# Gated product of a scan kernel: formed in token order in bf16 and transposed back, in place of an in-place fp32 product in PSUM

## The chip, the cores and the metric

One core of a Trainium2 chip runs the whole kernel. The metric is the device time of one execution in microseconds (us), the median of several. The profile is of one execution; its span is 1.7 to 1.8 us shorter than that execution's own time. PE is the matmul engine, DVE the vector engine, ACT the scalar engine with its function tables, POOL the general engine, SP the engine that issues most transfers.

## The reference, cut to what matters

```python
# x, r_gate, i_gate: (4, 6336, 256) fp32
a_t   = exp(8 * sigmoid(r_gate) * log(sigmoid(a_param)))
norm  = sqrt(max(1 - a_t * a_t, 1e-06))
x_gated = norm * sigmoid(i_gate) * x
for t in range(S):                       # one scan for each batch row and channel
    h = a_t[:, t] * h + x_gated[:, t]
    y[:, t] = h
# then: causal 5-tap convolution of y -> sigmoid gate; (gate * (y @ w_val)) @ w_out
```

The 25,344 tokens (4 x 6336) are cut into 51 tiles of up to 512 tokens and 28 chunks of up to two tiles. Inputs come with tokens on the partitions. The scan needs channels on the partitions and tokens along the free dimension, so something must be transposed; the change is about what, where and in which type.

## The kernel before

The parts that the change and the argument touch (cuts marked with `# ...`; h is one of two halves of the channels, k counts half chunks):

```python
UNITS = [1, 2, 2, 2, 2, 2, 3, 3, 2, 2, 2, 1, 1, 1, 2]   # chunks in one batch of square roots
OSB = "ADADAD..."   # who evicts output piece q from PSUM: D = DVE, A = ACT

def op_u2(g, eng):      # POOL: u = (tanh(i/2) + 1) * x, bf16, tokens on partitions
    # ...
def op_exp(k, eng):     # ACT: a = exp(..), read from PSUM transposed by PE, fp32
def op_e(k, eng):       # POOL: e = a * a
def op_sq(u, eng):      # ACT: norm = sqrt(0.25 - 0.25 e), bf16, one batch; needs another table
def op_uT(k, eng):      # PE: u transposed into the one fp32 PSUM buffer
    xg = psum.tile([P, CHUNK], FP32, name="xg", tag="xg", bufs=1)
    # ...
        nc.tensor.matmul(out=xg[:, o:o + (P - 1) * nj + 1:nj],        # stepped columns
                         lhsT=uring[:, g % NS, j, h * P:(h + 1) * P], rhs=ident_b[:], ...)
def op_xg(k, eng):      # DVE: product, in place
    nc.vector.tensor_tensor(out=xg[:, 0:nt], in0=xg[:, 0:nt], in1=nring[...], op=ALU.mult)
def op_scan(k, eng):    # DVE: reads a from SBUF and xg from PSUM, writes y
    nc.vector.tensor_tensor_scan(out=yring[...], data0=aring[...], data1=xg[:, c0:c1], ...)
```

Afterwards PE does the convolution (gp) and the value matmul (val), ACT the tanh of the gate (tg), DVE the gate product (gv), PE the output matmul (ops), and DVE or ACT the eviction (osb). A small list scheduler in the kernel (`make_plan`) fixes the order of all instructions from constants: a cost and a priority for each kind, the batches and the string of evictions. The change comes with its own set of these constants.

## Time and profile before

| | before |
|---|---|
| time, median of 3 | 351.11 us (350.84 to 351.58) |
| span of the profiled execution | 348.6 us |
| busy: ACT, DVE, POOL, PE | 310.3, 270.9, 266.6, 250.4 us |
| share of the load and store queue | 79.5% of 16 engines |

### The profile page before, as it was taken

How to read it: one execution, taken by the hardware profiler on the slowest of the kernel's cores; microseconds unless marked ns; L12 is line 12 of the kernel's file. 1: busy time of each engine (PE TensorE's matmuls, PEld its weight loads, DVE VectorE, ACT ScalarE, POOL GpSimd, SP SyncE). 2: the span in 40 equal slices, each digit the busy share in tenths (PEclk: the TensorE clock that was granted, in tenths of full speed). 3: DMA queues.
4: the chain of work that ended last, by engine and by line, in shares of the span. 5: the costliest groups of instructions: out<-in, count | busy, mean ns of one | idle time of the engine just before them, and what ended most of it. 6: DMA issues, size and time to landing. Idle time of an engine off the chain costs nothing.

```text
span 348.6 us, 6564 instructions
## 1 busy us (share of the span) xinstructions
PE 250.4 (72%) x2559; PEld 161.4 (46%) x2559; DVE 270.9 (78%) x247; ACT 310.3 (89%) x262; POOL 266.6 (76%) x170
## 2 busy tenths in 40 slices
PE   1162773796785986787687867849978866988884
PEld 0041441553453654554455554527545544555452
DVE  3031675587798899876989869976999989999992
ACT  6859999879899899889979989997999999999673
POOL 7788998999797997997799949967938965873200
PEclk9997598899897899998999989978999999999999
DMA  7997988895999978997999976996985996522324
GB/s 201 371 416 261 407 285 342 305 350 202 371 414 362 350 282 321 374 419 228 390 399 394 351 261 228 392 392 225 353 343 181 368 387 244 192 83 120 122 120 183
DMA packets 30797, 104.51 MB, mean 300 GB/s; under 512 B 4391, under 2 KB 4654, under 8 KB 30766
## 3 DMA queue, kind: packets, MB, share of 16 engines
q1 hardware_dynamic: 29390, 103.83, 79.5%
q0 software_dynamic: 1376, 0.26, 0.9%
q8 instruction: 20, 0.33, 0.4%
q14 instruction: 11, 0.09, 0.1%
HBM read 78.39 MB, written 25.95 MB: 299 GB/s over the span
## 4 chain that ended last, share of the span: by engine, by line
PE 31%; ACT 25%; DVE 16%; issue 13%; DMA 11%; POOL 2%; SPq 0%; DVEq 0%; ACTq 0%; POOLq 0%
PE gp L377 12%; PE xg L326 10%; DVE yring L351 8%; ACT tri L280 6%; DMA ri<-in_i_gate_dram 6%; ACT ering L315 5%; DVE xg L335 5%; ACT tg L385 4%; PE ops L415 4%; DMA wo<-in_moe_w_out_dram 4%; ACT L315 3%; PE val L393 3%; ACT L385 3%; PE srT L268 3%; ACT aring L302 2%
## 5 line engine op out<-in xcount | busy, mean ns | idle before, releaser
L310 POOL TENSOR_TENSOR ering<-aring 128x1024 f32<-128x1024 f32 (+2 forms) x56 | 94.5, 1694 | 45.1 <-ACT aring L302 42.6
L289 POOL TENSOR_TENSOR uring<-t,xt 128x1024 bf16<-128x1024 f32 (+1 forms) x51 | 117.0, 2294 | 4.2
L351 DVE TENSOR_TENSOR_SCAN yring<-aring,yring,xg 128x1024 bf16<-128x1024 f32 (+5 forms) x54 | 111.1, 2056 | 1.0
L280 ACT ACTIVATE tri<-ri 128x2048 bf16<-128x2048 f32 (+1 forms) x51 | 94.8, 1861 | 3.4 <-DMA ri<-in_i_gate_dram 3.3
L335 DVE TENSOR_TENSOR xg<-xg,ering 128x1024 f32<-128x1024 f32 (+2 forms) x56 | 62.0, 1107 | 43.3 <-PE xg L326 27.8
L326 PE MATMUL xg<-ident_b,uring 128*128 128x128 bf16 x396 | 58.8, 335 | 41.1 <-DVE yring L351 38.9
L377 PE MATMUL gp<-yring,diag 64*64 64x512 bf16 (+14 forms) x1164 | 72.0, 381 | 22.4 <-ACT tg L385 22.2
L302 ACT ACTIVATE aring<-srT,khf 128x1024 f32<-128x1024 bf16 (+2 forms) x56 | 62.0, 1108 | 9.4 <-PE srT L268 8.9
L326 PEld LDWEIGHTS <-uring 128*128 128x128 bf16 x396 | 44.4, 138 | 55.2 <-issue 44.1
L415 PE MATMUL ops<-wo,gv 128*128 128x256 bf16 x396 | 62.2, 279 | 10.5 <-DVE osb L426 5.1
L403 DVE SCALAR_TENSOR_TENSOR gv<-tg,val 128x1024 bf16<-128x1024 bf16 (+1 forms) x54 | 60.2, 1120 | 7.1 <-PE val L393 5.4
L287 POOL TENSOR_SCALAR t<-tri 128x1024 f32<-128x1024 bf16 (+1 forms) x51 | 52.0, 1019 | 11.9 <-ACT tri L280 10.5
L385 ACT ACTIVATE tg<-gp 128x1024 bf16<-128x1024 f32 (+1 forms) x51 | 51.0, 999 | 9.3 <-PE gp L377 8.9
L377 PEld LDWEIGHTS <-diag 64*64 64x64 bf16 x1164 | 32.3, 114 | 49.9 <-issue 36.8
L415 PEld LDWEIGHTS <-gv 128*128 128x128 bf16 x396 | 38.6, 105 | 32.1 <-issue 19.2
L393 PE MATMUL val<-yring,wv 128*128 128x512 bf16 (+1 forms) x204 | 51.8, 377 | 1.5 <-DVE gv L403 1.3
L315 ACT ACTIVATE ering<-ering,b 128x2048 bf16<-128x2048 f32 (+2 forms) x28 | 50.5, 1804 | 1.1
L268 PE MATMUL srT<-ident_b,tri 128*128 128x128 bf16 x396 | 35.1, 234 | 16.6 <-ACT aring L302 8.4
L426 DVE COPY osb<-ops 128x512 f32<-128x512 f32 x58 | 39.2, 676 | 7.6 <-PE ops L415 7.3
L268 PEld LDWEIGHTS <-tri 128*128 128x128 bf16 x396 | 28.8, 106 | 26.9 <-issue 13.7
L428 ACT COPY osb<-ops 128x512 f32<-128x512 f32 x41 | 24.0, 586 | 9.5 <-PE ops L415 9.2
L393 PEld LDWEIGHTS <-wv 128*128 128x128 bf16 x204 | 19.4, 99 | 16.8 <-issue 4.5
(29 smaller groups left out, 59.6 us busy)
## 6 DMA issues: line engine op xcount, KB each, us to landing
ri<-in_r_gate_dram SPq DMA_DIRECT2D x48, 512.0 KB, 6.2
ri<-in_i_gate_dram SPq DMA_DIRECT2D x48, 512.0 KB, 7.0
xt<-in_x_dram SPq DMA_DIRECT2D x48, 512.0 KB, 6.2
out_dram<-osb SPq DMA_DIRECT2D x48, 512.0 KB, 4.1
ri<-in_r_gate_dram SPq DMA_DIRECT2D x3, 256.0 KB, 3.1
ri<-in_i_gate_dram SPq DMA_DIRECT2D x3, 256.0 KB, 3.2
xt<-in_x_dram SPq DMA_DIRECT2D x3, 256.0 KB, 3.2
out_dram<-osb SPq DMA_DIRECT2D x3, 256.0 KB, 2.1
```

The costliest lines, as they stand in the source:

```text
L268: nc.tensor.transpose(out=dst[:, col:col + P], in_=src[:, j, h * P:(h + 1) * P], identity=ident_b[:])
L280: nc.scalar.activation(out=tri[:, :, 0:nj, :], in_=ri[:, :, 0:nj, :], func=ACT.Tanh, scale=0.5)
L289: nc.gpsimd.tensor_tensor(out=uring[:, g % NS, 0:nj, :], in0=t1[:, 0:nj, :], in1=xt[:, 0:nj, :], op=ALU.mult)
L310: nc.gpsimd.tensor_tensor(out=ering[:, h, a0:a0 + nt], in0=a, in1=a, op=ALU.mult)
L315: nc.scalar.activation(out=nring[:, :, 2 * a0:2 * a0 + nt], in_=ering[:, :, a0:a0 + nt], func=ACT.Sqrt, scale=-0.25, bias=b025[:, 0:1])
L326: nc.tensor.matmul(out=xg[:, o:o + (P - 1) * nj + 1:nj], lhsT=uring[:, g % NS, j, h * P:(h + 1) * P], rhs=ident_b[:], start=True, stop=True)
L335: nc.vector.tensor_tensor(out=xg[:, 0:nt], in0=xg[:, 0:nt], in1=nring[:, h, 2 * a0:2 * a0 + nt], op=ALU.mult)
L351: nc.vector.tensor_tensor_scan(out=yring[:, h, y0 + c0:y0 + c1], data0=aring[:, h, a0 + c0:a0 + c1], data1=xg[:, c0:c1], initial=0.0 if fr ...
L377: nc.tensor.matmul(out=gp[64 * h:64 * h + 64, m, c0:c1], lhsT=diag[rows, h, kk, rows], rhs=yring[rows, h, src:src + c1 - c0], start=(sh == 0),
L385: nc.scalar.activation(out=tg[:, :, 0:nt], in_=live.pop(("gp", g))[:, :, 0:nt], func=ACT.Tanh, scale=0.5)
L393: nc.tensor.matmul(out=val[:, m, 0:nt], lhsT=wv[:, hk, m * P:(m + 1) * P], rhs=yring[:, hk, y0:y0 + nt], start=(hk == 0), stop=(hk == H - 1))
L415: nc.tensor.matmul(out=ops[:, e, :], lhsT=gv[:, 2 * i + e, hk, :], rhs=wo2[:, hk, :], start=(hk == 0), stop=(hk == H - 1))
```

## The change

The intent is to shorten the product. The norm, computed with channels on the partitions, is transposed by PE to token order (bf16 in PSUM). There DVE multiplies it with u, bf16 with bf16 into bf16, a tile at a time. PE transposes the product back into bf16 PSUM, where the scan reads it. i and x must then be loaded with consecutive tokens on consecutive partitions, which turns runs of 4 KB in memory into runs of 1 KB. The batches of square roots are cut anew, the first of three chunks instead of one, the ring for y shrinks from 8 to 6 tiles, and evictions, costs and priorities are a new set.

```diff
-UNITS = [1, 2, 2, 2, 2, 2, 3, 3, 2, 2, 2, 1, 1, 1, 2]
+UNITS = [3, 1, 3, 3, 2, 3, 2, 3, 2, 2, 1, 1, 1, 1]
-NY = 8
+NY = 6
+NXG = 3
 # ... OSB: 41 evictions on ACT before, 32 after; COST and PRIO
-        for dst, src in ((ri[:, 0, 0:nj, :], rf), (ri[:, 1, 0:nj, :], if_), (xt[:, 0:nj, :], xf)):
-            nc.sync.dma_start(dst, src[t0:t0 + nt, :].rearrange("(p j) d -> p j d", j=nj))
+        nc.sync.dma_start(ri[:, 0, 0:nj, :], rf[t0:t0 + nt, :].rearrange("(p j) d -> p j d", j=nj))
+        for dst, src in ((ri[:, 1, 0:nj, :], if_), (xt[:, 0:nj, :], xf)):
+            nc.sync.dma_start(dst, src[t0:t0 + nt, :].rearrange("(j p) d -> p j d", p=P))
 # ... op_uT and the old op_xg go
+        def op_nT(g, eng):
+            # ...
+            nT = psum.tile([P, SUB, D], BF16, name="nT", tag="nT", bufs=1)
+                    nc.tensor.transpose(out=nT[:, j, h * P:(h + 1) * P],
+                                        in_=nring[:, h, n0 + j * P:n0 + (j + 1) * P], identity=ident_b[:])
+        def op_xg(g, eng):
+            xg = work.tile([P, SUB, D], BF16, name="xg", tag="xg", bufs=NXG)
+            nc.vector.tensor_tensor(out=xg[:, 0:nj, :], in0=live.pop(("nT", g))[:, 0:nj, :],
+                                    in1=uring[:, g % NS, 0:nj, :], op=ALU.mult)
+        def op_xT(k, eng):
+            xT = psum.tile([P, CHUNK], BF16, name="xT", tag="xT", bufs=1)
+            transposes(xT, [(live["xg", g], tiles[g][1] // P) for g in range(*chunks[c][2:])], h)
-                    ..., data1=xg[:, c0:c1],
+                    ..., data1=xT[:, c0:c1],
```

More of the change, by code (lines that the diff above doesn't have):

```diff
@@ L16 @@
 CHUNKS = [[256], [512]] + [[512, 512]] * 23 + [[512], [256], [256]]
-UNITS = [1, 2, 2, 2, 2, 2, 3, 3, 2, 2, 2, 1, 1, 1, 2]
+UNITS = [3, 1, 3, 3, 2, 3, 2, 3, 2, 2, 1, 1, 1, 1]
 NS = 10
-NY = 8
+NY = 6
 NIN = 3
 NTRI = 4
+NXG = 3
 NOSB = 3
-OSB = ("ADADADADDDDDDDDDDDDDDDDDDADADDDDDDDDADAAAADDDDDAADAADDDAADADDADADADADDAAAAADAAADADDADDDDAD"
-       "DAAAAAAAA")
+OSB = ("DDAADDDADDDDDDDDDDADADDDDDDDDADDADDDDDDDADDDDDDDADDDADDADAADADADADDDADDDDDADADADDAAAAAADDA"
+       "DDDDAAAAA")
 COST = dict(load=(0.1, 3.8), tanh=(0.2, 1.7), u2=(0.25, 3.15), srT=(0.05, 0.45), exp=(0.35, 0.86), e=(0.1, 1.8),
-            sq=(0.3, 1.71), uT=(0.1, 0.65), xg=(0.17, 1.07), scan=(0.21, 2.14), conv=(0.2, 1.1), tg=(0.19, 0.83),
+            sq=(0.3, 1.71), nT=(0.05, 0.47), xg=(0.1, 0.58), xT=(0.05, 0.45), scan=(0.21, 2.14), conv=(0.2, 1.1), tg=(0.19, 0.83),
             val=(0.02, 0.93), gv=(0.15, 1.07), out=(0.02, 0.47), osbD=(0.68, 0), osbA=(0.59, 0),
             store=(0.1, 1.2))
-PRIO = dict(load=5.13, store=-0.06, tanh=3.86, exp=-0.46, sq=-2, tg=-0.7, srT=0.17, uT=-2, conv=0.26, val=6,
-            out=-0.57, e=1.19, u2=4.62, xg=4.5, scan=6, gv=1.35, osb=-2)
+PRIO = dict(load=5.07, store=4.64, tanh=5.95, exp=3.94, sq=0.63, tg=0.73, srT=3.16, nT=4.77, xT=-1.91,
+            conv=3.92, val=4.01, out=-0.12, e=4.3, u2=4.55, xg=-0.64, scan=3.88, gv=4.0, osb=-0.43)
 TABLE, SEM, DMA_LAT = 1.3, 0.15, 2.2
@@ L93, in make_jobs @@
             + ([("srT", 2 * sh.chunk_of[g - NTRI] + 1)] if g >= NTRI else []))
-        job("u2", "POOL", f, [("tanh", g)] + ([("uT", 2 * sh.chunk_of[g - NS] + 1)] if g >= NS else []))
+        job("u2", "POOL", f, [("tanh", g)] + [("xg", g - NS)])
+        job("nT", "PE", f, [("sq", unit_of[c]), ("xg", g - 1)])
+        job("xg", "DVE", f, [("nT", g), ("u2", g)] + ([("xT", 2 * sh.chunk_of[g - NXG] + 1)] if g >= NXG else []))
         job("conv", "PE", f, [("scan", 2 * c + 1), ("tg", g - 1)])
@@ L109, in make_jobs @@
             job("e", "POOL", f, [("exp", k), aold])
-            job("uT", "PE", f, [("u2", g1 - 1), ("scan", k - 1)])
-            job("xg", "DVE", f, [("uT", k), ("sq", unit_of[c])])
-            job("scan", "DVE", f, [("xg", k), ("val", ylast - 1), ("conv", ylast)])
+            job("xT", "PE", f, [("xg", g1 - 1), ("scan", k - 1)])
+            job("scan", "DVE", f, [("xT", k), ("val", ylast - 1), ("conv", ylast)])
     for q, (g, i) in enumerate(sh.pieces):
@@ L316, in op_sq @@
                                      func=ACT.Sqrt, scale=-0.25, bias=b025[:, 0:1])
-        def op_uT(k, eng):
-            c, h = k // 2, k % 2
-            xg = psum.tile([P, CHUNK], FP32, name="xg", tag="xg", bufs=1)
-            g0, g1 = chunks[c][2:]
-            for g in range(g0, g1):
-                nj = tiles[g][1] // P
-                for j in range(nj):
-                    o = (g - g0) * WIN + j
-                    nc.tensor.matmul(out=xg[:, o:o + (P - 1) * nj + 1:nj],
-                                     lhsT=uring[:, g % NS, j, h * P:(h + 1) * P],
-                                     rhs=ident_b[:], start=True, stop=True)
-            live["xg", k] = xg
-        def op_xg(k, eng):
-            c, h = k // 2, k % 2
-            nt, a0 = chunks[c][1], shape.apos[c]
-            xg = live["xg", k]
-            nc.vector.tensor_tensor(out=xg[:, 0:nt], in0=xg[:, 0:nt], in1=nring[:, h, 2 * a0:2 * a0 + nt],
-                                    op=ALU.mult)
+        def op_nT(g, eng):
+            c = chunk_of[g]
+            n0 = 2 * shape.apos[c] + tiles[g][0] - chunks[c][0]
+            nT = psum.tile([P, SUB, D], BF16, name="nT", tag="nT", bufs=1)
+            for j in range(tiles[g][1] // P):
+                for h in range(H):
+                    nc.tensor.transpose(out=nT[:, j, h * P:(h + 1) * P],
+                                        in_=nring[:, h, n0 + j * P:n0 + (j + 1) * P], identity=ident_b[:])
+            live["nT", g] = nT
+        def op_xg(g, eng):
+            nj = tiles[g][1] // P
+            xg = work.tile([P, SUB, D], BF16, name="xg", tag="xg", bufs=NXG)
+            nc.vector.tensor_tensor(out=xg[:, 0:nj, :], in0=live.pop(("nT", g))[:, 0:nj, :],
+                                    in1=uring[:, g % NS, 0:nj, :], op=ALU.mult)
+            live["xg", g] = xg
+        def op_xT(k, eng):
+            c, h = k // 2, k % 2
+            xT = psum.tile([P, CHUNK], BF16, name="xT", tag="xT", bufs=1)
+            transposes(xT, [(live["xg", g], tiles[g][1] // P) for g in range(*chunks[c][2:])], h)
+            live["xT", k] = xT
         def yend(c):
@@ L348, in op_scan @@
             yp = yend(c) - 1
-            xg = live.pop(("xg", k))
+            xT = live.pop(("xT", k))
             for (c0, c1, fresh) in shape.segments(t0, nt):
                 nc.vector.tensor_tensor_scan(
-                    out=yring[:, h, y0 + c0:y0 + c1], data0=aring[:, h, a0 + c0:a0 + c1], data1=xg[:, c0:c1],
+                    out=yring[:, h, y0 + c0:y0 + c1], data0=aring[:, h, a0 + c0:a0 + c1], data1=xT[:, c0:c1],
                     initial=0.0 if fresh else yring[:, h, yp:yp + 1], op0=ALU.mult, op1=ALU.add)
@@ L436 @@
         ops_by_name = dict(load=op_load, tanh=op_tanh, u2=op_u2, srT=op_srT, exp=op_exp, e=op_e, sq=op_sq,
-                           uT=op_uT, xg=op_xg, scan=op_scan, conv=op_conv, tg=op_tg, val=op_val, gv=op_gv,
+                           nT=op_nT, xg=op_xg, xT=op_xT, scan=op_scan, conv=op_conv, tg=op_tg, val=op_val, gv=op_gv,
                            out=op_out, osb=op_osb, store=op_store)
```

## The prediction

> **What bounds the kernel now.** I read the page's first part, then the busy times by stretch, then the groups by shape, the waits, and last the chain in the stretch where the work of the vector engine looked tight. First the shares:
>
> ```profile
> span 348.6 us, 6564 instructions
> PE 250.4 (72%) x2559; PEld 161.4 (46%) x2559; DVE 270.9 (78%) x247; ACT 310.3 (89%) x262; POOL 266.6 (76%) x170
> ```
>
> ACT has least room: 38.3 us of idle in the span. The stretches (engine busy times in the order PE, PEld, DVE, ACT, POOL, then granted clock, DMA share, GB/s) tell when:
>
> ```profile
> 0.00:20.00 20.00, 3.63 (x19) 2.06 (x19) 4.87 (x20) 14.20 (x15) 14.03 (x21) 1.00 0.95 304
> 20.00:60.00 40.00, 21.30 (x180) 13.82 (x184) 18.37 (x17) 36.76 (x28) 37.58 (x22) 0.80 0.88 335
> ...
> 180.00:220.00 40.00, 31.81 (x359) 21.14 (x357) 35.16 (x29) 36.49 (x32) 33.36 (x20) 0.96 0.88 322
> 220.00:260.00 40.00, 31.27 (x313) 20.44 (x312) 35.19 (x27) 36.96 (x30) 28.46 (x18) 0.91 0.89 337
> 260.00:300.00 40.00, 31.45 (x361) 20.78 (x360) 37.41 (x30) 39.61 (x35) 30.38 (x18) 1.00 0.77 282
> 300.00:348.60 48.60, 38.72 (x414) 23.58 (x412) 40.07 (x43) 36.97 (x44) 16.57 (x15) 0.99 0.36 138
> ```
>
> ACT loses 5.8 us in the first 20, some 21 us spread over 20 to 300, and 11.6 at the end. Up to 60 us ACT and POOL are full and DVE idles; from 260 us on DVE is full too. So ACT sets the rate, and the scan stage on DVE, which started late, catches up with it. The groups by shape give unit costs:
>
> ```profile
> L335 DVE TENSOR_TENSOR xg<-xg,ering 128x1024 f32<-128x1024 f32 x46 | 56.6, 1230 | 31.7 <-PE xg L326 25.1 <-ACT ering L315 4.8 <-PE ops L415 0.9
> L326 PE MATMUL xg<-ident_b,uring 128*128 128x128 bf16 x396 | 58.8, 335 | 41.1 <-DVE yring L351 38.9 <-POOL t L287 1.5 <-POOL uring L289 0.6
> L426 DVE COPY osb<-ops 128x512 f32<-128x512 f32 x58 | 39.2, 676 | 7.6 <-PE ops L415 7.3
> L428 ACT COPY osb<-ops 128x512 f32<-128x512 f32 x41 | 24.0, 586 | 9.5 <-PE ops L415 9.2
> L315 ACT ACT_TABLE_LOAD x15 | 19.2, 1283 | 0.3
> ```
>
> The product waits 25 us for PE's placement, and PE waits 39 us for the scan: one buffer, two engines in turn. The chain in 281 to 313 us shows the loop (start, us, what):
>
> ```profile
> 290.33 1.05 PE xg L326 x8
> ...
> 291.46 1.25 DVE xg L335
> ...
> 292.73 2.36 DVE yring L351
> ...
> 295.13 1.05 PE xg L326 x8
> ```
>
> One half chunk takes 4.8 us there, and nothing in it belongs to ACT. So late in the kernel this loop is what ends last, and before that ACT is.
>
> **What the Trainium skill says.** (1) "VectorE: DVE Perf Modes", section "Why PSUM operands drop a tier": a PSUM operand limits an instruction to the packed mode with two 16-bit elements a cycle, and fp32 to one. The present product is fp32 and agrees: 429, 698 and 1230 ns at 256, 512 and 1024 elements are 1.04 ns an element plus 162 ns. But the tier table of the same page says 1x for a two-tensor instruction with any PSUM operand. No instruction of the trace before reads bf16 PSUM on DVE, so it can't decide. (2) "Advanced Engine Details and Errata", section "PSUM Cachelines": a non-contiguous pattern slows matmuls. The trace agrees: eight stepped placements took 1.03 us where eight contiguous transposes (srT) took 0.61; their medians were 314 and 219 ns. (3) "DMA: Bandwidth & Descriptors", section "Why small descriptors are slow (HBM only)": about 3 cycles a packet on top of one for each 32 bytes. No group in the trace isolates it. (4) "ScalarE: Activation LUTs", section "What ACT_TABLE_LOAD costs": about 1283 ns a load; the trace has 1283.
>
> **The change part by part.** *Product.* 56 products in fp32 go (62.0 us). 51 come, one a tile, bf16 PSUM and bf16 SBUF to bf16 SBUF. At two a cycle, a 1024 tile takes 162 + 1024 x 0.52 = 0.70 us, a 512 one 0.43 us: 48 x 0.70 + 3 x 0.43 = 34.9 us. DVE is relieved of 27 us. I choose the packed mode (about 85%), because the scarce thing the page names is ports, and each tensor here needs one.
>
> *Evictions.* By the two orders of instructions ACT's share of the 99 output copies falls from 41 to 32. DVE gains 9 x 0.676 = 6.1 us, ACT loses 9 x 0.586 = 5.3. *Batches.* 14 square-root batches for 15; the order shows 31 table loads for 33: ACT loses 2.6 us. Sums: DVE 270.9 - 27.1 + 6.1 = 250; ACT 310.3 - 7.9 = 302.4, about 303 since neighbouring instructions overlap a little.
>
> *PE.* 396 stepped placements go, 792 contiguous transposes come. From the groups of eight, less the last one's length, the spacing at full clock is (1.03 - 0.27)/7 = 0.109 us and (0.61 - 0.22)/7 = 0.056 us. So 43 us of issue go and 44 come: neutral, though PE's busy figure, which adds up latencies (219 ns each), would rise by some 50 to 60 us less overlap.
>
> *The loop.* The product leaves it: transposes 0.6, scan 2.36, a little over 0.1 for semaphores, 3.1 us where there were 4.8. DVE can form later products and evict while PE transposes. Per full chunk DVE needs 4 x 2.34/2 for two scans = 4.7, two gates 2.4, two products 1.4, and 67/99 of four copies 1.8: 10.3 us. ACT needs about 303/24.75 = 12.2 us. So ACT stays the bound, now with 2 us a chunk in hand.
>
> *Buffers and start.* The first square root waits for three chunks where it waited for one, so the first scan moves from 18 us to some 30; but before, the second batch began only at 34 us (DVE waited 8.9 us for it), so that costs little. At the end each batch has norm transposes and product transposes in series, about 1 us more.
>
> *Sum.* ACT busy 303; start 5; its waits of 21 us in the middle, which come from transposes, gates and outputs late by that loop, I put at 15; the end 12. That is a span of 335, and with the 2.5 us between span and time, 337.5. I say **338 us**, 3.7% faster.
>
> **Rivals.** *A, the packed mode fails.* Then a product costs 1.23 us; DVE gets 51 x 0.53 = 26 us back, 276 us, above before. For it: the tier table. Against: the port argument. The time would be 348 to 356.
> *B, the loads become the bound.* Two of three loads now land token by token: 1 KB runs for 4 KB, 13,056 packets become 50,688. By the skill's cycles four 1 KB packets take 4 x 35 = 140 where one of 4 KB takes 131: 7% on half the bytes, an estimate. The DMA share up to 300 us was 0.88, so it becomes 0.91, and 0.94 at the faster pace. For it: a chain already passes through an i_gate load for 10.5 us at 139 us. Against: ACT waited for loads only 3.3 us in all, and three buffers run ahead; the issuing queue itself waited 71 us for POOL to free them. Time 343 to 350.
> *C, ACT alone counts.* The loop is hidden, its waits persist elsewhere (PE works in order, and three kinds of transposes can block srT). Then only the 8 us of ACT go: 343.
> *D, all waits go.* ACT nearly dense from 10 us: 328.
>
> **Range and chances.** The centre is 338; D sets the low end at 327, and B or C together with some loss at the start the high end at 349. Faster by 2% means under 344.1. A has 15%, strong B 10%, C lies near the border: faster 0.70, within 2% 0.25, slower 0.05 (A together with a bad start).
>
> **What would show it.** Product group: 48 at 0.70 us (right) or 1.23 (A). DVE near 250, ACT near 303 busy, ACT's share above 90%. PE's wait for the scan well under 39 us, DVE's wait for PE under 20. Load time to landing little above 6 to 7 us; if ACT waits for loads over 8 us, B is at work. The forecast fails if the product stays at one a cycle, if ACT's idle stays at 38 us, or if POOL, unchanged at 264 us and more, turns up as the last waiter in the first 200 us.

## More of the kernel before

The shares are averages over the whole span. What they hide is the distribution in time, and that turns out to matter: two lines of the stretches view cut the span of before at 100 us. The columns are the stretch, its length, then PE, PEld, DVE, ACT, POOL busy, then granted clock, DMA share and GB/s.

```profile
0.00:100.00 100.00, 55.66 (x499) 35.91 (x500) 53.51 (x61) 87.06 (x69) 87.90 (x63) 0.88 0.89 323
100.00:348.60 248.60, 194.78 (x2062) 125.44 (x2060) 217.36 (x187) 223.21 (x194) 178.74 (x108) 0.96 0.78 290
```

DVE does only 53.5 us of work in the first 100 and 217.4 us in the remaining 248.6.

## The result

| | before | after |
|---|---|---|
| time, median of 4 each in the same rounds | 350.98 us (349.21 to 351.58) | 339.10 us (338.72 to 340.38) |
| ratio of the fast runs | 1 | 0.9676 (95% interval 0.9632 to 0.972) |
| span of the profiled execution | 348.6 us | 338.6 us |

Executions over 1.5% slower than the fastest of the same kernel are left out of the means. Ratios here and below are the mean time of one kernel's fast runs over that of the other's in the same rounds, so they are not quite the ratio of the medians quoted beside them. The result is right by the reference. The forecast of 338 us was 1.1 us off.

The busy times of the page for the kernel after:

```profile
PE 252.6 (75%) x2987; PEld 166.9 (49%) x2987; DVE 247.2 (73%) x251; ACT 302.8 (89%) x251; POOL 266.5 (79%) x170
```

DVE lost 23.7 us of work and ACT 7.5, close to the 21 and 7 to 8 us worked out before. PE's busy time rose by only 2 us. The stretches of the kernel after, in the columns explained above:

```profile
0.00:20.00 20.00, 3.17 (x19) 1.92 (x19) 3.32 (x17) 11.78 (x12) 14.00 (x21) 1.00 0.97 273
20.00:60.00 40.00, 21.84 (x230) 14.52 (x231) 17.98 (x19) 34.33 (x26) 36.06 (x22) 0.96 0.98 333
60.00:100.00 40.00, 25.03 (x249) 17.80 (x250) 17.70 (x18) 36.66 (x27) 36.96 (x22) 0.71 0.99 346
100.00:140.00 40.00, 36.06 (x426) 23.36 (x425) 35.37 (x34) 35.06 (x28) 33.45 (x20) 0.90 0.88 299
140.00:180.00 40.00, 33.15 (x402) 21.91 (x401) 35.73 (x34) 37.64 (x28) 38.54 (x23) 1.00 1.06 376
180.00:220.00 40.00, 31.20 (x407) 21.73 (x407) 33.54 (x31) 38.51 (x30) 34.58 (x21) 0.91 1.00 344
220.00:260.00 40.00, 35.70 (x444) 23.55 (x433) 35.77 (x34) 39.75 (x35) 36.15 (x21) 1.00 1.02 358
260.00:300.00 40.00, 34.86 (x440) 22.56 (x443) 36.97 (x37) 39.76 (x34) 28.60 (x18) 1.00 0.80 289
...
300.00:338.60 38.60, 31.57 (x396) 19.60 (x388) 30.84 (x33) 29.30 (x37) 8.18 (x10) 0.97 0.34 137
```

Three things are to be seen. ACT idles 8.2 us in the first 20, and 9.3 us at the end (38.6 less 29.3); the rest of its 35.8 us of idle, 18.3 us, lies between. DVE is emptier from 60 to 100 us (17.7 us) than before the change, where the finer stretches have 30.3 us; the granted clock of PE there is 0.71, and it was 0.90. And the DMA share is 0.97 to 1.06 in every stretch up to 260 us but one (0.88 from 100 to 140); before the change it was 0.86 to 0.95.

The groups of the kernel after (columns as in the prediction's group lines; the product is now L335 with other operands):

```profile
L335 DVE TENSOR_TENSOR xg<-nT,uring 128x1024 bf16<-128x1024 bf16 x48 | 32.5, 678 | 20.0 <-POOL uring L293 9.7 <-PE nT L328 5.4 <-POOL ering L314 3.9
```

The product runs at 678 ns for 1024 elements against the 1230 ns that the prediction showed for the fp32 product: the packed mode works with one operand in PSUM. The waits of the kernel after (who waited for whom: us in total, times, longest us):

```profile
DVE xg L335 <- PE nT L328: 26.4, 9, 20.9
DVE yring L358 <- PE xT L272: 11.3, 12, 3.0
ACT tri L284 <- DMA ri<-in_i_gate_dram: 9.3, 7, 2.4
PE xT L272 <- DVE yring L358: 6.3, 8, 1.4
```

PE's wait for the scan fell from 38.9 us to 6.3, so most of the waiting in that loop of two engines is gone. One wait of 20.9 us at the start is the price of the first batch of three chunks. ACT waits longer for loads. Late in the kernel DVE runs almost without gaps (36.97 us of work in the 40 from 260 us on), but so does ACT (39.76). The chain that ended last, in shares of the span by engine, of the changed kernel and of a_stt, a run told below in which only DVE's product is longer:

```profile
PE 28%; ACT 23%; DVE 18%; DMA 17%; issue 12%; SPq 2%; ACTq 0%; DVEq 0%
```

```profile
DVE 36%; PE 27%; issue 14%; ACT 11%; DMA 9%; SPq 2%; DVEq 0%; ACTq 0%
```

In the changed kernel no engine dominates the chain, so it was not clear from this alone that ACT still sets the rate, as the prediction has it. The same cut at 100 us as shown for before:

```profile
0.00:100.00 100.00, 50.05 (x496) 34.23 (x497) 39.00 (x53) 82.77 (x64) 87.02 (x63) 0.87 0.98 326
100.00:338.60 238.60, 202.53 (x2492) 132.71 (x2490) 208.22 (x199) 220.03 (x187) 179.49 (x108) 0.96 0.85 301
```

After 100 us DVE is busy 208.2 of 238.6 us, 87.3%. Before the change it was 217.4 of 248.6, 87.4%. DVE shed 23.7 us of work in all, but it does 14.5 us less of it in the first 100 us (39.0 against 53.5), so only 9.1 us less remains for the rest; at 87.3% that is 10.5 us, and the span shrank by 10.0. As the two shares are almost equal, this sum fits whatever the cause, so it is a hint and not a test. It suggested a second theory.

### The profile page after: what moved, and what is told of

Read it like the earlier page. It is cut to its first block, busy times and chain, and to the rows that moved or that the text cites. A ratio compares the mean times of both kernels' runs of the same rounds, so it can differ in the third digit from the quotient of the medians.

```text
span 338.6 us, 7417 instructions
## 1 busy us (share of the span) xinstructions
PE 252.6 (75%) x2987; PEld 166.9 (49%) x2987; DVE 247.2 (73%) x251; ACT 302.8 (89%) x251; POOL 266.5 (79%) x170
## 4 chain that ended last, share of the span: by engine, by line
PE 28%; ACT 23%; DVE 18%; DMA 17%; issue 12%; SPq 2%; ACTq 0%; DVEq 0%
DMA ri<-in_i_gate_dram 14%; PE gp L384 10%; DVE yring L358 8%; ACT tri L284 6%; PE ops L422 5%; PE val L400 4%; ACT tg L392 4%; DVE gv L410 4%; ACT ering L319 4%; DVE osb L433 4%; PE xT L272 4%; ACT aring L306 3%; PE srT L272 3%; PE nT L328 2%; ACT L392 2%
## 5 line engine op out<-in xcount | busy, mean ns | idle before, releaser
L358 DVE TENSOR_TENSOR_SCAN yring<-aring,yring,xT 128x1024 bf16<-128x1024 f32 (+5 forms) x54 | 111.1, 2057 | 11.5 <-PE xT L272 10.8
L384 PE MATMUL gp<-yring,diag 64*64 64x512 bf16 (+16 forms) x1196 | 71.4, 363 | 9.3 <-ACT tg L392 7.9
L422 PE MATMUL ops<-wo,gv 128*128 128x256 bf16 x396 | 60.8, 277 | 10.2 <-DVE osb L433 6.2
L335 DVE TENSOR_TENSOR xg<-nT,uring 128x1024 bf16<-128x1024 bf16 (+1 forms) x51 | 33.8, 662 | 40.9 <-PE nT L328 26.4
L392 ACT ACTIVATE tg<-gp 128x1024 bf16<-128x1024 f32 (+1 forms) x51 | 51.3, 1006 | 5.0 <-PE gp L384 4.8
L433 DVE COPY osb<-ops 128x512 f32<-128x512 f32 x67 | 45.6, 680 | 13.9 <-PE ops L422 13.8
L272 PEld LDWEIGHTS <-tri 128*128 128x128 bf16 x396 | 27.9, 105 | 44.5 <-ACT tri L284 23.7
L422 PEld LDWEIGHTS <-gv 128*128 128x128 bf16 x396 | 36.1, 99 | 26.1 <-issue 15.6
L328 PE MATMUL nT<-ident_b,ering 128*128 128x128 bf16 x396 | 34.3, 235 | 12.8 <-ACT ering L319 7.6
L272 PE MATMUL xT<-ident_b,xg 128*128 128x128 bf16 x396 | 34.7, 231 | 8.7 <-DVE yring L358 6.3
L272 PEld LDWEIGHTS <-xg 128*128 128x128 bf16 x396 | 27.0, 103 | 22.0 <-issue 14.8
L328 PEld LDWEIGHTS <-ering 128*128 128x128 bf16 x396 | 27.8, 106 | 19.3 <-ACT ering L319 8.9
## 6 DMA issues: line engine op xcount, KB each, us to landing
ri<-in_r_gate_dram SPq DMA_DIRECT2D x3, 256.0 KB, 4.6
ri<-in_i_gate_dram SPq DMA_DIRECT2D x3, 256.0 KB, 6.0
xt<-in_x_dram SPq DMA_DIRECT2D x3, 256.0 KB, 4.8
out_dram<-osb SPq DMA_DIRECT2D x3, 256.0 KB, 2.0
```

Of the source, the lines that this page charges most:

```text
L272: nc.tensor.transpose(out=dst[:, col:col + P], in_=src[:, j, h * P:(h + 1) * P], identity=ident_b[:])
L328: nc.tensor.transpose(out=nT[:, j, h * P:(h + 1) * P], in_=nring[:, h, n0 + j * P:n0 + (j + 1) * P], identity=ident_b[:])
L358: nc.vector.tensor_tensor_scan(out=yring[:, h, y0 + c0:y0 + c1], data0=aring[:, h, a0 + c0:a0 + c1], data1=xT[:, c0:c1], initial=0.0 if fr ...
L384: nc.tensor.matmul(out=gp[64 * h:64 * h + 64, m, c0:c1], lhsT=diag[rows, h, kk, rows], rhs=yring[rows, h, src:src + c1 - c0], start=(sh == 0),
L392: nc.scalar.activation(out=tg[:, :, 0:nt], in_=live.pop(("gp", g))[:, :, 0:nt], func=ACT.Tanh, scale=0.5)
L422: nc.tensor.matmul(out=ops[:, e, :], lhsT=gv[:, 2 * i + e, hk, :], rhs=wo2[:, hk, :], start=(hk == 0), stop=(hk == H - 1))
```

## The experiments

**Theory 1** is the prediction's: ACT sets the rate, DVE has room, and the gain is ACT's relief plus shorter waits. **Theory 2**: from about 100 us on, the scan stage (DVE, with PE feeding it) sets the end, and what counts is how much of DVE's work is left then. **Theory 3**: loads with short runs, or POOL, hold the front back. Twelve kernels were run, four to a chip, each against the kernel before on the same chip; the changed kernel itself was not run again in these rounds. All kernels named a_ are edits of the changed kernel (0.9676, 339.1 us), those named b_ of the kernel before.

### ACT without its table loads (a_one_table)

```diff
-                                     func=ACT.Sqrt, scale=-0.25, bias=b025[:, 0:1])
+                                     func=ACT.Tanh, scale=-0.25, bias=b025[:, 0:1])
```

> The changed kernel with tanh in place of the square root (wrong result on purpose), so that no batch needs another table: table loads from 31 to 3, which takes 36 us from ACT and leaves everything else. If ACT is the bound: 312 to 322 us, ACT busy about 267. If loads or POOL stand right behind ACT: 325 to 332 us, with ACT waiting longer for loads. If DVE is the bound: 336 us or more.

Measured: 331.75 us (328.87 to 332.47), ratio 0.9456 (0.9392 to 0.9519). Its output is wrong, which doesn't matter for the time. ACT's busy time fell by 36.3 us to 266.5, the time by only some 7.5 us. Theory 1 predicted 312 to 322 us and fails: four fifths of ACT's relief is not passed on. The reading for DVE as the bound, 336 us or more, was missed too. The time lies in the range of the middle reading, loads or POOL right behind ACT, and ACT did wait longer for the i_gate load (13.7 us for 9.3). The cut at 100 us:

```profile
0.00:100.00 100.00, 55.24 (x554) 37.71 (x559) 44.54 (x55) 77.91 (x61) 91.31 (x66) 0.88 1.02 339
100.00:330.70 230.70, 195.62 (x2400) 127.84 (x2428) 202.42 (x197) 188.60 (x163) 175.22 (x105) 0.96 0.86 306
```

DVE did 44.5 us by 100 us instead of 39.0, and is busy 88% of the rest. So the run also fits theory 2, if ACT's relief only lets the scan stage begin earlier; the reading for DVE had not allowed for that. The DMA share of 1.02 fits loads behind ACT as well.

### ACT and POOL both relieved (a_table_pool)

```diff
-            t1 = work.tile([P, SUB, D], FP32, name="t1", tag="t1", bufs=1)
-            nc.gpsimd.tensor_scalar(out=t1[:, 0:nj, :], in0=tri[:, 1, 0:nj, :], scalar1=1.0, scalar2=1.0,
-                                    op0=ALU.mult, op1=ALU.add)
-            nc.gpsimd.tensor_tensor(out=uring[:, g % NS, 0:nj, :], in0=t1[:, 0:nj, :], in1=xt[:, 0:nj, :],
+            nc.gpsimd.tensor_tensor(out=uring[:, g % NS, 0:nj, :], in0=tri[:, 1, 0:nj, :], in1=xt[:, 0:nj, :],
 # ... and Tanh for Sqrt as in a_one_table
```

> As a_one_table (tanh in place of the square root, wrong result on purpose, 331.75 us) with POOL's first pass over u left out as well (52 us of POOL, also wrong on purpose). If POOL was what stood behind ACT in a_one_table: 305 to 320 us. If the loads did: 326 to 331 us, with the DMA share of the load queue above 89% and ACT waiting longer for loads. If the scan stage did (DVE, PE): 326 to 331 us with no longer waits for loads.

Measured: 329.27 us (327.29 to 329.87), ratio 0.9401 (0.936 to 0.9441). Its output is wrong, which doesn't matter for the time. POOL lost 62.4 us of busy time (266.5 to 204.1) beside ACT's 36.7, and the time fell by about 2 us more, with intervals that overlap. POOL is not behind ACT. The load queue's share was 89.0%, as in a_one_table (89.1%), and ACT's wait for the i_gate load 12.3 us against 13.7 there, so the "loads" reading asked for more than the run showed. But ACT still waited longer than in the changed kernel (9.3), and the DMA share was 1.00 to 1.06 from 20 to 260 us but for 0.88 from 100 to 140. Loads right behind ACT are not ruled out. The next section asks what the short runs cost in the changed kernel itself.

### Loads in long runs again (a_runs4k)

```diff
-            nc.sync.dma_start(dst, src[t0:t0 + nt, :].rearrange("(j p) d -> p j d", p=P))
+            nc.sync.dma_start(dst, src[t0:t0 + nt, :].rearrange("(p j) d -> p j d", j=nj))
```

> The changed kernel with the i and x loads in runs of 4 KB again (as before the change). Result wrong on purpose: tokens of u no longer match those of the norm; instructions, order and sizes are the same. Theory (ACT sets the rate, the short runs cost a little): packets 68,432 to about 30,800, DMA share of the load queue from 87.6% to about 80%, ACT's wait for the i_gate load from 9.3 us to 3 to 5 us, time 334 to 337 us. Rival (loads became the real bound): 326 to 332 us. Rival (loads wholly hidden): 338 to 340 us.

Measured: 336.43 us (334.53 to 337.59), ratio 0.9602 (0.9552 to 0.9652). Its output is wrong, which doesn't matter for the time. The queue lines of the pages of before, after and a_runs4k, in this order (packets, MB, share of 16 engines over the span):

```profile
q1 hardware_dynamic: 29390, 103.83, 79.5%
```

```profile
q1 hardware_dynamic: 67022, 103.83, 87.6%
```

```profile
q1 hardware_dynamic: 29390, 103.83, 82.7%
```

Multiplied with the spans, the queue was at work for 277, 297 and 278 us. The short runs cost 19.5 us of it, or 312 us of single engines for 37,632 more packets: 8.3 ns a packet. On the time, long runs gave back 2.7 us by the medians (0.76% by the ratios, whose intervals overlap), with ACT's wait for loads down from 9.3 to 5.1 us. Short runs are a small cost, as the first reading had it, and the load queue alone does not bound the changed kernel. Fewer bytes, or long runs together with ACT's relief, were not tried.

### A product that is not packed (a_stt, and first a_unpacked)

The first try read and wrote all three operands in crossed order, so that neighbours lie 128 elements apart:

```diff
+            def cross(v):
+                return v.rearrange("c j (h p) -> c j p h", h=H)
-            nc.vector.tensor_tensor(out=xg[:, 0:nj, :], in0=live.pop(("nT", g))[:, 0:nj, :],
-                                    in1=uring[:, g % NS, 0:nj, :], op=ALU.mult)
+            nc.vector.tensor_tensor(out=cross(xg[:, 0:nj, :]), in0=cross(live.pop(("nT", g))[:, 0:nj, :]),
+                                    in1=cross(uring[:, g % NS, 0:nj, :]), op=ALU.mult)
```

> The changed kernel with the product's three operands read and written in crossed order (step of 128 elements), so that two neighbours are no longer adjacent. Same values, right result. Both theories: 1.2 us a product of 1024 instead of 0.68, DVE busy from 247 to about 274 us. If the gain is owed to the product leaving the loop of transposes and scan (DVE has room to spare): 339 to 343 us. If it is owed to DVE's shorter busy time: 347 to 353 us, back at the time before.

Measured: 530.3 us (528.17 to 534.24), ratio 1.5152, result right. The group line shows that the edit did much more than take the packing away:

```profile
L337 DVE TENSOR_TENSOR xg<-nT,uring 128x1024 bf16<-128x1024 bf16 x48 | 225.3, 4693 | 19.2 <-PE nT L328 18.0 <-POOL t L291 0.6 <-POOL ering L314 0.2
```

At 4.7 us for 1024 elements it is nearly four times the 1.2 us that both readings had expected, so this run does not decide between them. The second try uses the three-operand instruction of the gate, with the same operands, buffers and order:

```diff
-            nc.vector.tensor_tensor(out=xg[:, 0:nj, :], in0=live.pop(("nT", g))[:, 0:nj, :],
-                                    in1=uring[:, g % NS, 0:nj, :], op=ALU.mult)
+            nc.vector.scalar_tensor_tensor(out=xg[:, 0:nj, :], in0=live.pop(("nT", g))[:, 0:nj, :], scalar=1.0,
+                                           in1=uring[:, g % NS, 0:nj, :], op0=ALU.mult, op1=ALU.mult)
```

> The changed kernel with the product formed by the three-operand instruction that the gate uses (times 1.0, times u), same operands, buffers and order of all instructions. Right result. Expected of the instruction: one element a cycle, 1.15 to 1.25 us for a 1024 tile instead of 0.68 (the product of before took 1.23). DVE busy 247 to about 273 us, as much as before the change, but with the product still out of the loop of transposes and scan. If the gain is owed to the shorter product: 347 to 353 us. If it is owed to the loop and ACT: 339 to 343 us. Halfway: 344 to 346.

Measured: 353.34 us (352.48 to 355.69), ratio 1.0119 (1.0076 to 1.0161), result right. Its product group and its cut at 100 us:

```profile
L335 DVE SCALAR_TENSOR_TENSOR xg<-nT,uring 128x1024 bf16<-128x1024 bf16 x48 | 58.1, 1211 | 19.4 <-PE nT L328 16.1 <-POOL ering L314 3.1 <-issue 0.2
```

```profile
0.00:100.00 100.00, 51.07 (x493) 35.52 (x494) 44.05 (x52) 82.18 (x64) 86.55 (x63) 0.86 0.98 323
100.00:353.90 253.90, 209.24 (x2497) 133.91 (x2494) 228.59 (x199) 222.43 (x188) 180.38 (x108) 0.95 0.81 284
```

The product takes 1211 ns, as long as before the change, and stays outside the loop. DVE's busy time rose by 25.4 us to 272.6, and the time by about 14 us (4.4 points of the ratio, or 15.5 us): the whole gain is lost and a little more. After 100 us DVE has 228.6 us of work in 253.9, 90%, and DVE's share of the chain that ended last rose from 18% to 36%. The time lies just above the range for a gain owed to the shorter product (347 to 353 us) and far from the other (339 to 343), in which DVE had room for these 25 us. PE's wait for the product before the norm's transposes, which share one buffer, rose from 5.1 to 10.5 us, so a part of the loss may be that wait. The planned order is the one made for the short product; a set of constants searched for the long one might do better, which was not tried.

### Evictions moved, order kept (a_copies_back, a_copies_dve)

These two keep the plan and change only which engine does some evictions (the plan is made with the old string, the work is given out by a second one, DOES):

```diff
-            if eng == "DVE":
+            if DOES[q] == "D":
```

In a_copies_back, 9 evictions spread over the kernel go from DVE to ACT; in a_copies_dve, 17 go from ACT to DVE.

> The changed kernel with 9 of its output copies, spread over the kernel, done by ACT instead of DVE (41 on ACT as before the change), while the planned order of everything stays. Right result. ACT busy 303 to 307 to 308, DVE 247 to 241 us. If ACT's busy time is the bound and its relief part of the gain: 342 to 345 us. If not: 338 to 340 us.

> The changed kernel with 17 of ACT's output copies (numbers 15 to 79) done by DVE while the planned order of everything stays, unlike a_osb_d, where the order moved too. Right result. ACT busy 303 to about 294, DVE 247 to 258 us. If ACT is the bound and DVE has room: 331 to 336 us, better than both kernels. If loads or POOL stand right behind ACT: 336 to 339. If it is as slow as a_osb_d (350 us), DVE has no room, and the order was not to blame.

Measured: a_copies_back 349.60 us (347.89 to 350.45), ratio 0.9995 (0.9955 to 1.0034); a_copies_dve 348.93 us (348.6 to 349.2), ratio 0.9981 (0.9958 to 1.0004). Both results are right, and both edits cost about 10 us, in opposite directions of load. In a_copies_dve ACT had 6.4 us less work and DVE 10.7 us more; DVE's share after 100 us was 217.8 of 246.8 us, 88%. The time is that of a_osb_d, the sign that DVE has no room; but the output matmul's wait for DVE's evictions also rose, from 6.2 to 20.4 us. In a_copies_back DVE had 3.6 us less work, and its share after 100 us fell to 202.8 of 246.1, 82%: its eviction instructions waited 23.9 us for PE's output matmul instead of 13.8, and that matmul waited 13.2 us for ACT's evictions instead of 3.6. There is one output buffer in PSUM, and ACT evicts only when its turn in the planned order comes. So a_copies_back missed both of its readings: 4.7 us more on ACT do not explain a loss of 10, and the waits point to the place of these copies in ACT's order. Evictions moved within a fixed order cost time in either direction, so these two runs do not tell DVE's load from that order.

### One part of the set of constants alone (a_osb_d, a_osb_b, a_units_b, b_osb_a)

Here a constant is exchanged and the plan is made anew with it:

```diff
 # a_osb_d: 17 evictions (numbers 15 to 79) of OSB from A to D
 # a_osb_b: OSB of the kernel before, in the changed kernel
 # b_osb_a: OSB of the changed kernel, in the kernel before
 # a_units_b:
-UNITS = [3, 1, 3, 3, 2, 3, 2, 3, 2, 2, 1, 1, 1, 1]
+UNITS = [1, 2, 2, 2, 2, 2, 3, 3, 2, 2, 2, 1, 1, 1, 2]
```

> The changed kernel with 17 more of the output copies (numbers 15 to 79, those left to ACT) on DVE: ACT copies from 32 to 15, ACT busy 303 to about 293, DVE 247 to about 259 us. Right result. If ACT is still the bound and DVE has room: 332 to 337 us, better than both kernels. If DVE's room is in the wrong places (start and end) or loads hold ACT up anyway: 338 to 342 us.

> The changed kernel with the split of the output copies of the kernel before (41 on ACT instead of 32). Right result. ACT busy 303 to about 308, DVE 247 to 241 us. If ACT sets the rate and the moved copies are part of the gain: 341 to 345 us. If the loop alone made the gain: 338 to 340 us.

> The changed kernel with the batches of square roots of the kernel before (15, the first of one chunk). Right result. Table loads 31 to 33 or so, first scan at about 18 to 20 us instead of 35. If the batches are part of the gain (ACT): 341 to 344 us. If the late first scan costs as much as the table loads give: 337 to 341 us.

> The kernel before with the changed kernel's split of output copies (32 on ACT instead of 41) and nothing else. Right result. ACT busy 310 to 305, DVE 271 to 277 us. If ACT alone counts: 345 to 348 us. If the scan loop on DVE counts as well, so that the copies could only be moved once the product got cheap: 351 to 358 us.

| run | time, us | ratio (95%) | DVE busy to 100 us | DVE busy after, of | share |
|---|---|---|---|---|---|
| a_osb_d | 351.64 | 1.0042 (0.9973 to 1.0111) | 40.9 | 216.1 of 248.6 | 87% |
| a_osb_b | 358.10 | 1.0217 (1.0148 to 1.0286) | 40.3 | 201.9 of 256.0 | 79% |
| a_units_b | 352.80 | 1.0082 (1.0013 to 1.0151) | 51.3 | 198.0 of 251.2 | 79% |
| b_osb_a | 356.79 | 1.0185 (1.0138 to 1.0233) | 54.7 | 221.3 of 252.5 | 88% |

All four results are right. In two of them the loss is far from what busy times explain: against the changed kernel DVE's work fell by 5.0 us in a_osb_b and rose by 2.2 in a_units_b (in a_osb_d it rose by 9.9). a_osb_b lost 19 us where I expected 2 to 6, a_units_b 14 where I expected 0 to 5, a_osb_d 12 where I hoped for a gain. Only b_osb_a lies in its expected range, that of the reading in which the scan stage on DVE counts. A constant cannot be lifted out of its set: another string reorders instructions on all engines, and the two runs with 79% show DVE waiting, not working: theory 2 does not account for them, nor for a_copies_back with 82%. It follows that these four runs cannot price one part of the set. a_units_b shows one thing more: an early start alone (51.3 us of DVE work by 100 us) does not make the kernel fast.

### The loop broken in the kernel before (b_split)

```diff
-            nc.vector.tensor_tensor(out=xg[:, 0:nt], in0=xg[:, 0:nt], in1=nring[:, h, 2 * a0:2 * a0 + nt],
+            xs = work.tile([P, CHUNK], BF16, name="xs", tag="xs", bufs=2)
+            nc.vector.tensor_tensor(out=xs[:, 0:nt], in0=xg[:, 0:nt], in1=nring[:, h, 2 * a0:2 * a0 + nt],
 # the scan reads xs; in the plan uT waits for the product instead of the scan, the product for the scan two back
```

> The kernel before with the product written to a bf16 buffer in SBUF instead of in place, so that PE may place the next half chunk while DVE scans: the loop is broken, the product keeps its length (1.23 us), loads stay in 4 KB runs, batches and copies as before. Right result. Both: PE's wait for the scan from 39 us to under 12 us, DVE's wait for PE's placement from 28 us to under 15. If breaking the loop is a large part of the gain: 341 to 346 us. If the waits only hid behind ACT: 348 to 352 us.

Measured: 403.53 us (400.91 to 404.27), ratio 1.1525, result right: a miss of both readings. The waits in question went down or away (in the profile PE's placement waits 29.0 us, now for the product and no longer for the scan). But the scan now has two inputs in SBUF. The groups on POOL of before, then of b_split:

```profile
L289 POOL TENSOR_TENSOR uring<-t,xt 128x1024 bf16<-128x1024 f32 x48 | 113.2, 2358 | 4.0
...
L287 POOL TENSOR_SCALAR t<-tri 128x1024 f32<-128x1024 bf16 x48 | 50.1, 1044 | 10.2 <-ACT tri L280 8.8 <-PE srT L268 0.3
```

```profile
L289 POOL TENSOR_TENSOR uring<-t,xt 128x1024 bf16<-128x1024 f32 x48 | 133.6, 2783 | 4.0
...
L287 POOL TENSOR_SCALAR t<-tri 128x1024 f32<-128x1024 bf16 x48 | 91.1, 1899 | 8.5 <-ACT tri L280 3.9 <-DMA out_dram<-osb 3.7
```

The same POOL instructions take 2783 instead of 2358 ns and 1899 instead of 1044 ns, POOL's busy time grows from 266.6 to 347.5 us, and the scan itself from 2342 to 2951 ns. "Advanced Engine Details and Errata" of the Trainium skill, section "GPSIMD Details", says that POOL shares a read and a write interface with DVE and conflicts with DVE instructions that have two SBUF inputs; the numbers here agree with it and give its size. So b_split can't tell what breaking the loop is worth. It does show a price that the changed kernel avoids, as its scan reads the product from PSUM.

No variant beat the changed kernel with a right result.

## Why the prediction was right or wrong

**Right in the number, in part by luck.** 338 us was forecast and 339.1 measured, inside the range. The sum behind it stands on ACT as the bound, which the runs do not bear out.

**Right: unit costs.** The packed product (0.70 us forecast, 0.678 measured), DVE's busy time (250, 247.2), ACT's (303, 302.8), and the end of the loop of two engines (PE's wait for the scan 38.9 to 6.3 us). The choice between two statements of the skill's page on DVE fell for the packed mode, and that choice carried the result: a_stt, the changed kernel without packing in the same order, is 1.2% slower than the kernel before.

**Wrong: the bound.** The step that failed is "So ACT stays the bound, now with 2 us a chunk in hand". Taking 36.3 us from ACT gave 7.5 us; taking another 62.4 us from POOL gave some 2; giving DVE 25.4 us took 14 to 15.5. Per microsecond of work the time follows DVE about three times as closely as ACT, though one is work added and the other work taken away. So the room on DVE that the step counted on, about 2 us a chunk or nearly 50 us in all, is not there: these 25 us would have fitted into it. That DVE is what binds the changed kernel is argued and not shown, since no run took work from the changed kernel's DVE without moving it to ACT. The likely mistake was an average: DVE's 10.3 us for each chunk was spread over the whole span, while DVE does only 39 us of its 247 in the first 100 us and must fit 208 into the 239 that remain. The prediction had read "from 260 us on DVE is full too" and then priced the change as if that were not so. Rival A, the product at one element a cycle, had 348 to 356 us, which a_stt met at 353.3 (the rival's sum has a slip: 51 x 0.53 is 27 and not 26); that rival contradicted the main line, and I did not notice.

**Wrong: the sum of ACT's idle.** It came out because its terms missed in both directions: start 5 forecast and 8.2 measured, middle 15 and 18.3, end 12 and 9.3. A sum of an engine's busy and idle time equals the span whatever the cause, so that it nearly fits says nothing for ACT as the cause. Two of the signs missed or nearly so: ACT's share is 89% and not above 90%, and its idle time 35.8 us, nearer to the 38 us that was to count as failure than to the 32 forecast. The 2.5 us between span and time compared a median with another execution's span; within one execution it is 1.8.

**Mis-sized: the late first scan.** "That costs little" was wrong in size. The first product waited until 34.3 us, DVE's longest wait 20.9 us, and with the slower front up to 100 us DVE had 14.5 us less done there than before. By the account above, this took back more than half of the 23.7 us that DVE saved. That account is read from two traces and is not the outcome of an experiment, and the lower granted clock from 60 to 100 us (0.71 for 0.90) was not separated from the batches; a_units_b, which starts early again, loses the time in other waits.

**Mis-sized: the loads.** The prediction put 3.5% more work on the load queue, from about 3 cycles a packet; it was 7% (277 to 297 us), 8.3 ns for each extra packet. "If ACT waits for loads over 8 us, B is at work": it waits 9.3, and a_runs4k puts the price at about 2.7 us, not the 5 to 12 us of that rival.

**Wrong in a detail: PE.** Its busy time was to rise by up to 50 or 60 us and rose by 2; the two new groups have 69.0 us of busy time where the old one had 58.8. The busy figure does not add up latencies: the prediction's own line has 396 placements of 335 ns, 133 us in sum, in 58.8 us. That it is neutral was right. The stepped placements and the contiguous transposes also differ in the type that they write (fp32, bf16), so the trace before did not isolate the step. DVE's wait for PE was to fall under 20 us; it is 26.4 for the norm's transposes and 11.3 for the product's, and under 20 only without the 20.9 us at the start.

**Open.** What binds the changed kernel was not settled. From 100 to 260 us ACT and DVE are busy 84% to 99% and the DMA share is 0.88 to 1.06, and relief of ACT (36.3 us gave 7.5) or of the load queue (19.5 gave 2.7) was tried one at a time; ACT and loads together were not. From the changed kernel to a_stt the time rose 0.6 us for each us of DVE's work, and from there to a_unpacked (441.4 us busy, 530.3 us) about one for one, which fits a DVE that is not yet the only limit in the changed kernel. Nor was it settled why DVE is at 87% after 100 us and not higher. PE is at 202.5 of 238.6 us there, 85%, and the two feed each other through single buffers; no run separated them. It is not known either what breaking the loop alone is worth, as b_split brought a new conflict, or what a set of constants searched for a_stt would give.

## What to carry to other kernels

Cut a span where an engine's load changes before averaging over it: an engine with 73% in all can lack room later, because it could not start early. An engine is a bound only if relieving it helps, so test by taking work away (which was done here for ACT, POOL and the loads, but not for DVE), and distrust a sum of busy and idle time that fits. When a tuned order is part of a kernel, do not exchange one constant of it alone. Holding the order fixed is cleaner but not clean: it was made for the old lengths and engines.

## What the Trainium skill lacked or had wrong

- "VectorE: DVE Perf Modes", section "The perf-mode tier table (the rule you actually need)": it gives 1x for a two-tensor instruction with any PSUM operand. With bf16 in PSUM, bf16 in SBUF and bf16 out, 1024 elements took 678 ns, with bf16 and fp32 in PSUM 1230 ns; the packed mode works, as a later section of the same page has it.
- The same table has no row for the three-operand instruction (scalar_tensor_tensor): with the same bf16 operands it took 1211 ns for 1024 elements, so no packed mode showed.
- "Vector Engine (DVE) Microarchitecture Reference", section "5.2 Measured stream behaviour on trn2 (trn3 not measured)", gives the cost of stepped operands for 4-byte elements in SBUF, up to 2.51 ns an element, but not for bf16 or PSUM: with a step of 128 elements in all three operands, 1024 elements of bf16, one operand in PSUM, took 4693 ns, 4.6 ns each. Which operand costs most was not separated.
- "Advanced Engine Details and Errata", section "GPSIMD Details", names the conflict of POOL with a DVE instruction with two SBUF inputs but not its size: POOL's instructions grew from 1044 to 1899 ns and from 2358 to 2783, the scan from 2342 to 2951 ns on average.
- "DMA: Bandwidth & Descriptors", section "Why small descriptors are slow (HBM only)": the 3 cycles a packet, by estimate 3.5 ns at the 850 MHz that the page gives in another section, understate the cost of runs of 1 KB instead of 4 KB in this mix of transfers, which was 8.3 ns a packet.
